# Two small evictions and a negation moved from ScalarE to VectorE in a fused convolution and gated MLP with gradients

## The chip, the cores and the metric

The kernel runs on one core of one Trainium2 chip, in one launch. The time is the device time in microseconds. Before the change it is 517.62 us, the median of three runs (517.49 to 518.38). A core has five engines that run side by side, each through its own instructions in order: TensorE (PE in the profile, with its weight loads as PEld), VectorE (DVE), ScalarE (ACT), GpSimd (POOL) and SyncE (SP, which here only starts transfers).

## The reference

The kernel computes one forward pass and the gradients of nine of its inputs. Sequence length S is 2048, width D is 512, inner width F is 1376, all in bf16.

```
xn = layernorm(A_q)
k_shift[t] = sum over lag 0..3 of k[t - lag] * shift_k[:, lag]
kv = k_shift * v
y  = causal convolution of kv with ssm_k along S (FFT of length 4096) + kv * ssm_D
s  = xn * y
h  = sigmoid(xn @ w_gate) * (xn @ w_up)
g  = silu(h @ w_down)
out = A_q + s * g
```

It returns `out` and, for a given `grad_out`, the gradients for A_q, A_k, A_v, A_shift_k, A_ssm_k, A_ssm_D, w_gate, w_up and w_down. The gradients of the convolution are convolutions as well, so they need a forward transform of the gradient of `y`, products with the spectra of `kv` and `ssm_k`, and inverse transforms.

## The kernel before

**Tiles.** The sequence is cut into NJ = 16 tiles of 128 positions, and position p * 16 + j lies on partition p of tile j. The width is cut into 4 groups of 128 channels (`cg`). The tiles go through the MLP in the order SEQ, which begins 15, 13, 11, 9; `POS[i]` is the place of tile i in it, so `POS[i] < 2` means tiles 15 and 13.

**Stages.** In the first stage (up to about 160 us) four streams are interleaved: `strG` runs the gate and up projections of nine tiles (`f_gen`), `strK` and `strV` make the spectra of `ssm_k` and `kv`, and `strX` multiplies them and transforms back. The second stage (`stepB`, up to about 355 us) does the rest of the MLP and its backward pass, tile by tile. In the last stage `frontC` transforms the gradient of `y`, `backC` makes the two products and their inverse transforms for each channel group, and `dW` computes the three weight gradients as long accumulations of matmuls (into PSUM tiles of their own), which fill TensorE between the others.

**A tile's projections.** `f_ln` computes a tile's statistics on VectorE with a power on GpSimd, and writes the normalised tile to `xnA`. `f_xt` transposes it: for the places 0 to 3 and 9 to 11 of SEQ with four 128x128 matmuls against the identity into a PSUM tile of the kind "tr", of which there are two, then an eviction to `xnT` (line 732); for the others with a DMA. `f_gen` multiplies the weights with `xnT` in three blocks of 32, 32 and 24 matmuls. The projections of tile 15 wait for the weights, which are loaded in three pieces; the first block of tile 13 uses the same first piece as that of tile 15.

**An eviction.** `evac` (line 238) records a copy from PSUM to SBUF with two alternatives, ScalarE or VectorE.

**The last stage's spectra.** For each group and each quarter `qq` of its channels `step3T` makes a spectrum by two matmuls into a PSUM tile of 1024 columns (two banks), with the real parts on one half of the partitions and the imaginary parts on the other. From it come two SBUF tiles: `Xc`, the spectrum itself (`dst`), and `Xw`, the same with the halves swapped and one negated (`sw`). In this stage such 1024-wide PSUM tiles come from two slots (kind "mm2c"), which all steps of the transforms share. A slot is free once its last reader is done. Lines 958 to 960:

```python
        nc.evac(v(dst), pv[:], 1024)
        nc.scalar.copy(v(sw[0:64]), pv[64:128])
        nc.scalar.mul(v(sw[64:128]), pv[0:64], -1.0)
```

`backC` then makes four products on VectorE (lines 1353 to 1355), for t = 0 and 1: `PP[t]` from `Xc`, and `KK[t]` from `Xw`, in place over the loaded spectra. Two `inv3` calls follow, each of 16 matmuls: the first takes `PP[0]` and `KK[0]`, the second `PP[1]` and `KK[1]`.

**What sets the order.** No instruction is issued where it is written. The class `Rec` records all of them, the streams being interleaved by `run_streams` by shares of their work. `order` then plays the whole program through a cost model of the engines, the transfers and the PSUM slots, and gives each engine its order: of the operations that are ready, the one that was recorded first goes first. At the same place it chooses the engine of an eviction, VectorE only if ScalarE is behind by a margin. So a changed cost or a fixed engine at one place changes the order and the choices at many later ones. All instructions are emitted on line 522, which is why every line of the profile names it; groups are told apart by engine, operation and shape.

Of the kernel before, what the change touches and what calls it, by code (L numbers as in the profile page):

```python
# [9 lines left out]
ALU = mybir.AluOpType  # L10
# [27 lines left out]
POS = {i: n for n, i in enumerate(SEQ)}  # L38
# [598 lines left out]
def kernel_impl(ctx, tc, A_q, A_k, A_v, A_shift_k, A_ssm_k, A_ssm_D, B_x, B_w_gate, B_w_up, B_w_down,  # L637
                grad_out, out_0, out_1, out_2, out_3, out_4, out_5, out_6, out_7, out_8, out_9):
    nc = tc.nc
# [18 lines left out]
    def ps_mm(shape, dt=f32, name=None):  # L658
        return nc.ps(PS["mm"], shape, dt)
# [4 lines left out]
    def ps_tr(shape, dt=bf16, name=None):  # L664
        return nc.ps("tr", shape, dt)
# [25 lines left out]
    T = [dict() for _ in range(NJ)]  # L691
# [31 lines left out]
    def f_xt(i):  # L723
        if POS[i] > 3 and not 8 < POS[i] < 12:
            T[i]["xnT"] = xnT_r.next()
            nc.sync.dma_start_transpose(T[i]["xnT"], xnA[:, i, :])
            return
        pt = ps_tr([4, 128], name="ps_xnT")
        for db in range(4):
            nc.tensor.transpose(pt[:, db, :], xnA[:, i, db * 128:(db + 1) * 128], ident)  # L730
        T[i]["xnT"] = xnT_r.next()
        nc.evac(T[i]["xnT"], pt[:], 512)

    def f_gen(i):
        xnT = T[i]["xnT"]
# [129 lines left out]
    f_ln(SEQ[0])  # L865
    next(consts)
    f_xt(SEQ[0])
    f_ln(SEQ[1])
    next(consts)
# [74 lines left out]
    def step3T(Qf, rows, qq, dst, sw):  # L944
        if rows:
            ps = ps_mm([64, 8, 2], name="ps_x")
            for h in range(2):
                src = Qf.rearrange("p (k g) -> p k g", g=64)[:, 32 * h:32 * h + 32, 16 * qq:16 * qq + 16]
                nc.tensor.matmul(ps[:, 32 * h:32 * h + 32].rearrange("p k g x -> p k (g x)"), BDq, src, start=True, stop=True)
            pv = ps.rearrange("p k g x -> p g k x")  # L950
            v = lambda a: a.rearrange("p (g k x) -> p g k x", g=8, x=2)
        else:
            pv = ps = ps_mm([1024], name="ps_x")
            for h in range(2):
                o = 1024 * qq + 512 * h
                nc.tensor.matmul(ps[:, h * 512:(h + 1) * 512], BDq, Qf[:, o:o + 512], start=True, stop=True)
            v = lambda a: a
        nc.evac(v(dst), pv[:], 1024)
        nc.scalar.copy(v(sw[0:64]), pv[64:128])
        nc.scalar.mul(v(sw[64:128]), pv[0:64], -1.0)  # L960

    def inv3(parts, qq, Bg, rows=False):
        ps = ps_mm([8, NJ, 8], name="ps_b")
# [346 lines left out]
    def ld_KK(n):  # L1310
        if n < 16:
            KK = KK_r.next()
            nc.sync.dma_start(KK, KK_d[n // 4, n % 4].rearrange("t p x -> p t x"))
            stC["KK", n] = KK
# [10 lines left out]
    def ld_bwd(cg):  # L1325
        c0, c1 = cg * GW, (cg + 1) * GW
        if cg % 2 == 0:
            stC["vg"] = vg_r.next()
            nc.sync.dma_start(stC["vg"], vC[:, :, c0:c0 + 256])
        ksh, kh = ksh_r.next(), kh_r.next()  # L1330
        nc.sync.dma_start(ksh.rearrange("p j d -> p (j d)"), ksh_d[cg])
        nc.gpsimd.memset(kh[0:1, 0:3, :], 0.0)
        nc.sync.dma_start(kh[:, 3:, :], kC[:, :, c0:c1])
        ld_halo(nc.sync, kh[:, 0:3, :], kHalo[:, 0:3, c0:c1])
        stC["bwd", cg] = (ksh, kh)

    def backC():
        for cg in range(NG):
            c0, c1 = cg * GW, (cg + 1) * GW
            B1, B2 = B1_r.next(), B2_r.next()  # L1340
            ys = {}
            for qq in range(5):
                if qq < 4:
                    n = cg * 4 + qq
                    while ("Qf", cg) not in stC:
                        yield 0
                    Xc, Xw = Xc_r.next(), Xw_r.next()
                    step3T(stC["Qf", cg], cg > 1, qq, Xc, Xw)
                    stC["nY"] = n + 1
                    yield 1024  # L1350
                    KK = stC.pop(("KK", n))
                    PP = P_r.next()
                    for t in range(2):
                        nc.vector.tensor_tensor(PP[:, t], Xc, KK[:, t], ALU.mult)
                        nc.vector.tensor_tensor(KK[:, t], Xw, KK[:, t], ALU.mult)
                    ys[qq] = (PP, KK)
                if qq == 2:
                    ld_bwd(cg)
                if qq > 0:
                    PP, KK = ys.pop(qq - 1)  # L1360
                    inv3([(PP[:, 0], RC1), (KK[:, 0], RS2)], qq - 1, B1)
                    yield 2048
                    inv3([(PP[:, 1], RC1), (KK[:, 1], RS2)], qq - 1, B2, True)
                    ld_KK(cg * 4 + qq + 2)
                    yield 2048
            dkv = y2A[:, :, c0:c1]
            yield from inv1(B1, dkv)
            ksh, kh = stC.pop(("bwd", cg))
            vg = stC["vg"][:, :, (cg % 2) * GW:(cg % 2 + 1) * GW]
            dks = dks_r.next()  # L1370
            nc.vector.tensor_tensor(dks[:, 0:NJ, :], dkv, vg, ALU.mult)
            nc.vector.memset(dks[96:P, NJ:NJ + 3, :], 0.0)
            nc.gpsimd.dma_start(dks[0:112, NJ:NJ + 3, :], dks[1:113, 0:3, :])
            nc.gpsimd.dma_start(dks[112:127, NJ:NJ + 3, :], dks[113:128, 0:3, :])
            nc.vector.tensor_tensor(dkv, dkv, ksh, ALU.mult)
            dKT = ar.view(B1_r.blks[0][0], [128, NJ], bf16)
            Bv = B2.rearrange("p j e g c -> p j (e g) c")
            for jh in range(2):
                pk = ps_mm([8, 128], name="ps_dk")
                for jj in range(8):  # L1380
                    j = 8 * jh + jj
                    for c in range(2):
                        nc.tensor.matmul(pk[:, jj, :], Bv[:, j, :, c], Ci[:, c, j, :], start=(c == 0), stop=(c == 1))
                nc.evac(dKT[:, :, 8 * jh:8 * jh + 8], pk[:].rearrange("p j n -> p n j"), 1024)
                yield 2048
            nc.sync.dma_start(out_5[c0:c1, :], dKT.rearrange("p n j -> p (n j)"))
            if cg % 2 == 1:
                nc.sync.dma_start(o3C[:, :, c0 - GW:c1], y2A[:, :, c0 - GW:c1])
            nc.vector.tensor_copy(dDo[:, cg:cg + 1], dKT[:, 0, 0:1])
            pa = ps_tr([4, 32], f32, name="ps_diag")  # L1390
            for j in range(NJ):
                for e in range(4):
                    es = slice(32 * e, 32 * e + 32)
                    nc.tensor.matmul(pa[es], dks[:, j, es], kh[:, j:j + 4, es], start=(j == 0), stop=(j == NJ - 1))
                if j == 7:
                    yield 2048
            nc.vector.tensor_tensor(dm, pa[:], id32[:, None, :].to_broadcast([P, 4, 32]), ALU.mult)
            nc.vector.tensor_reduce(res[:, cg, :], dm, AX.X, ALU.add)
            yield 2048
            if cg % 2 == 0:  # L1400
                stC["dk"] = dk_r.next()
            dk = stC["dk"][:, :, (cg % 2) * GW:(cg % 2 + 1) * GW]
            for lag in range(4):
                src = dks[:, lag:lag + NJ, :]
                skl = skb[:, lag:lag + 1, c0:c1].to_broadcast([P, NJ, GW])
                if lag == 0:
                    nc.vector.tensor_tensor(dk, src, skl, ALU.mult)
                else:
                    term = term_r.next()
                    nc.vector.tensor_tensor(term, src, skl, ALU.mult)  # L1410
                    yield 512
                    nc.vector.tensor_tensor(dk, dk, term, ALU.add)
                yield 512
            if cg % 2 == 1:
                nc.sync.dma_start(o2C[:, :, c0 - GW:c1], stC["dk"])
        for lag in range(4):
            nc.vector.tensor_copy(skout[:, :, lag:lag + 1], res[:, :, 3 - lag:4 - lag])
        po = ps_tr([GW, 4], f32)
        for t in range(4):
            nc.tensor.matmul(po[0:4, :, t], skout[:, :, t], ident, start=True, stop=True)  # L1420
        nc.evac(row4[0:4, :], po[0:4].rearrange("p a t -> p (a t)"), 512)
        nc.sync.dma_start(out_4.rearrange("(g p) t -> g (p t)", p=P), row4[0:4, :])
        pd = ps_tr([GW], f32)
        nc.tensor.matmul(pd[0:4, :], dDo, ident, start=True, stop=True)
        nc.evac(row6[0:4, :], pd[0:4], 128)
        nc.sync.dma_start(out_6.rearrange("(g p) -> g p", p=P), row6[0:4, :])
# [116 lines left out]
```

## Time and profile before

| | |
|---|---|
| time | 517.62 us |
| span of the profiled run | 516.4 us |
| TensorE busy | 489.1 us, 95% |
| VectorE busy | 387.6 us, 75% |
| ScalarE busy | 353.2 us, 68% |
| GpSimd busy | 136.7 us, 26% |
| granted TensorE clock | 1.0 |
| data moved | 112.92 MB, 219 GB/s |
| ScalarE, negation of a half spectrum, 64x1024 f32 from PSUM | 16, 1.015 us each |
| ScalarE, copy of a half spectrum, 64x1024 f32 from PSUM | 16, 1.008 us each |
| ScalarE, eviction of 128x1024 f32 in the last stage | 69, 1.024 us each |
| VectorE, eviction of 128x1024 f32 in the last stage | 7, 1.219 us each |
| VectorE, product 128x1024 bf16 in the last stage | 64, 0.687 us each |

The busy time of an engine is the time in which at least one of its instructions ran. A group's line gives the engine, the operation, what it writes and reads, the shapes, the count, the busy time and the mean of one, and then the idle time just before these instructions with what ended it. A stretch in the timeline is a run of instructions without a gap; the idle time before it stands in brackets. Loss on an engine counts only where TensorE, or what it waits for, is held up by it.

### The profile page before, as it was taken

The numbers are of one execution on the slowest core, as the hardware profiler recorded it, in microseconds if no ns is written. First come the engines' busy times: TensorE is split into PE (matmuls) and PEld (weight loads), VectorE is DVE, ScalarE is ACT, GpSimd is POOL, SyncE is SP. The second block draws the span as 40 slices with busy tenths as digits, with TensorE's granted clock in tenths as the row PEclk, the third lists the DMA queues.
The fourth block names the chain that finished last, engine by engine and source line by source line (L and its number), as shares of the span: only waits on it lengthen the run. The fifth ranks groups of instructions, "written<-read, shape, count | busy, mean of one in ns | idle before, by whom it ended". The sixth has DMA issues, their size and how long they took to land.

```text
span 516.4 us, 13503 instructions
## 1 busy us (share of the span) xinstructions
PE 489.1 (95%) x5379; PEld 350.0 (68%) x5437; DVE 387.6 (75%) x768; ACT 353.2 (68%) x471; POOL 136.7 (26%) x257
## 2 busy tenths in 40 slices
PE   4789899899899999999999999999999999999997
PEld 3678798889787676666666556644675675866644
DVE  8799998877648779867779998436759859698440
ACT  7799999988975564455545546326878988786611
POOL 7255634444413432424153511000010010010000
PEclk9999999999999999999999999999999999999999
DMA  8989996698999655737499956989699699999973
GB/s 208 310 265 282 317 329 211 189 289 193 218 200 211 176 171 135 222 110 196 115 244 233 243 181 164 231 286 235 149 218 268 175 268 300 211 242 240 211 200 100
DMA packets 176888, 112.92 MB, mean 219 GB/s; under 512 B 126587, under 2 KB 160985, under 8 KB 176570
## 3 DMA queue, kind: packets, MB, share of 16 engines
q1 hardware_dynamic: 164424, 76.54, 63.5%
q0 software_dynamic: 11872, 35.53, 21.9%
q8 instruction: 42, 0.69, 0.6%
q14 instruction: 20, 0.16, 0.1%
q10 hardware_dynamic: 530, 0.01, 0.1%
HBM read 37.65 MB, written 45.72 MB: 161 GB/s over the span
## 4 chain that ended last, share of the span: by engine, by line
PE 77%; ACT 9%; DVE 7%; issue 4%; DMA 2%; POOL 1%; ACTq 0%; DVEq 0%; POOLq 0%
PE psum L522 77%; ACT slab L522 9%; DVE slab L522 7%; DMA slab<-in_A_q_dram 1%; DMA slab<-in_A_ssm_D_dram 1%; POOL slab L522 1%; POOL hF_d L522 0%; ACTq L522 0%; DVEq L522 0%; POOLq L522 0%
## 5 line engine op out<-in xcount | busy, mean ns | idle before, releaser
L522 PE MATMUL psum<-slab 128*128 128x128 bf16 (+4 forms) x5379 | 489.1, 254 | 24.2 <-ACT slab L522 10.1
L522 PEld LDWEIGHTS <-slab 128*128 128x128 bf16 (+1 forms) x5437 | 350.0, 99 | 163.0 <-issue 15.8
L522 DVE TENSOR_TENSOR slab<-slab 128x512 bf16<-128x512 bf16 (+6 forms) x488 | 268.9, 601 | 53.1 <-ACT slab L522 45.8
L522 ACT CAST slab<-psum 128x1024 bf16<-128x1024 f32 (+5 forms) x276 | 224.5, 867 | 91.1 <-PE psum L522 81.4
L522 ACT ACTIVATE slab<-psum 128x512 bf16<-128x512 f32 (+2 forms) x80 | 55.2, 694 | 38.9 <-PE psum L522 35.6
L522 ACT ACTIVATE slab<-slab 128x512 bf16<-128x512 bf16 (+3 forms) x71 | 56.8, 810 | 15.2 <-DVE slab L522 13.9
L522 ACT COPY slab<-psum 128x1024 bf16<-128x1024 bf16 (+1 forms) x42 | 39.2, 987 | 13.5 <-PE psum L522 13.5
L522 POOL DMA_DIRECT2D out_dram<-slab x32 | 17.4, 545 | 95.4 <-DVE slab L522 95.4
L522 POOL DMA_DIRECT2D slab<-slab x8 | 4.3, 544 | 130.9 <-DVE slab L522 130.6
L522 DVE TENSOR_TENSOR slab<-psum,slab 128x512 bf16<-128x512 f32 (+2 forms) x47 | 29.4, 627 | 10.6 <-ACT slab L522 7.7
L522 POOL DMA_DIRECT2D hF_d<-slab x48 | 26.2, 547 | 30.7 <-DVE slab L522 30.0
L522 DVE SCALAR_TENSOR_TENSOR slab<-psum,slab 128x512 bf16<-128x512 f32 x16 | 11.1, 691 | 27.1 <-PE psum L522 27.1
L522 DVE CAST slab<-psum 128x1024 bf16<-128x1024 f32 (+1 forms) x18 | 20.2, 1131 | 4.1 <-PE psum L522 4.0
L522 POOL DMA_DIRECT2D KK_d<-slab x32 | 17.4, 546 | 17.0 <-ACT slab L522 15.5
L522 POOL DMA_DIRECT2D slab<-in_A_q_dram x29 | 16.1, 556 | 11.0 <-DVE slab L522 4.8
L522 DVE SCALAR_TENSOR_TENSOR slab<-slab 128x512 bf16<-128x512 bf16 (+3 forms) x41 | 17.1, 416 | 0.8
L522 DVE STREAM_TRANSPOSE slab<-slab 128x1024 f32<-128x1024 f32 x8 | 14.3, 1834 | 4.0 <-ACT slab L522 4.0
L522 DVE TENSOR_SCALAR slab<-slab 128x1 f32<-128x1 f32 (+9 forms) x48 | 12.1, 268 | 6.3 <-POOL slab L522 5.4
L522 POOL TENSOR_TENSOR slab<-slab 128x1 f32<-128x1 f32 x16 | 9.8, 615 | 14.0 <-DVE slab L522 13.8
L522 POOL DMA_DIRECT2D slab<-hF_d x18 | 9.7, 541 | 12.2 <-PE psum L522 10.1
L522 DVE BATCH_NORM_STATS2 slab<-slab 128x6 f32<-128x512 bf16 x16 | 10.9, 686 | 0.5 <-DMA slab<-in_A_q_dram 0.5
L522 POOL DMA_DIRECT2D slab<-in_grad_out_dram x16 | 8.6, 540 | 7.6 <-DMA out_dram<-slab 7.1
(23 smaller groups left out, 48.9 us busy)
## 6 DMA issues: line engine op xcount, KB each, us to landing
KK_d<-slab POOLq DMA_DIRECT2D x32, 256.0 KB, 5.0
slab<-KK_d SPq DMA_DIRECT2D x16, 512.0 KB, 4.7
slab<-in_A_k_dram SPq DMA_DIRECT2D x8, 512.0 KB, 6.3
hF_d<-slab POOLq DMA_DIRECT2D x32, 128.0 KB, 4.0
slab<-slab SPq DMA_DIRECT2D x32, 128.0 KB, 4.7
out_dram<-slab POOLq DMA_DIRECT2D x32, 128.0 KB, 3.1
uF_d<-slab SPq DMA_DIRECT2D x32, 128.0 KB, 2.4
gF_d<-slab SPq DMA_DIRECT2D x32, 128.0 KB, 2.6
```

Source lines behind the costliest of these rows:

```text
L522: getattr(getattr(self.nc, eng), meth)(*[place(v) for v in a], **{x: place(v) for x, v in k.items()})
```

## The change

Three edits. The eviction of the transposed activations of the first two tiles is fixed to VectorE, in place of the planner's choice (before, ScalarE evicted tile 15 and VectorE tile 13). The negated half of `Xw` is made by VectorE from `Xc` in SBUF, in place of ScalarE from PSUM: it takes work from ScalarE and makes the half copy the last reader of the PSUM tile beside the eviction. And the two products that need only `Xc` are recorded ahead of the two that need `Xw`, so that VectorE has something to do while the swapped half is made.

```diff
@@ f_xt
         T[i]["xnT"] = xnT_r.next()
-        nc.evac(T[i]["xnT"], pt[:], 512)
+        if POS[i] < 2:
+            nc.vector.tensor_copy(T[i]["xnT"], pt[:])
+        else:
+            nc.evac(T[i]["xnT"], pt[:], 512)
@@ step3T
         nc.evac(v(dst), pv[:], 1024)
         nc.scalar.copy(v(sw[0:64]), pv[64:128])
-        nc.scalar.mul(v(sw[64:128]), pv[0:64], -1.0)
+        nc.vector.tensor_scalar(sw[64:128], dst[0:64], -1.0, None, ALU.mult)
@@ backC
                     for t in range(2):
                         nc.vector.tensor_tensor(PP[:, t], Xc, KK[:, t], ALU.mult)
+                    for t in range(2):
                         nc.vector.tensor_tensor(KK[:, t], Xw, KK[:, t], ALU.mult)
```

## The prediction

> **What bounds the kernel now.** I read the page's busy shares first, then the busy time of the engines stage by stage, then TensorE's stretches and waits in the places that the change touches.
>
> ```profile
> PE 489.1 (95%) x5379; PEld 350.0 (68%) x5437; DVE 387.6 (75%) x768; ACT 353.2 (68%) x471; POOL 136.7 (26%) x257
> ```
>
> TensorE is busy for 489.1 of 516.4 us, so all that can be won by moving work between the other engines is its 27.3 us of idleness. The stage table says where that lies (columns: stretch, its length, busy us of PE, PEld, DVE, ACT, POOL).
>
> ```profile
> 0.00:40.00 40.00, 28.31 (x355) 24.12 (x358) 34.21 (x84) 32.54 (x44) 21.49 (x45) 1.00 0.95 264
> 40.00:80.00 40.00, 37.31 (x580) 33.89 (x585) 37.28 (x53) 39.99 (x49) 19.40 (x35) 1.00 0.92 299
> 80.00:120.00 40.00, 37.64 (x588) 34.19 (x590) 33.58 (x50) 36.41 (x44) 17.36 (x33) 1.00 0.77 230
> 120.00:160.00 40.00, 36.90 (x558) 32.86 (x562) 24.20 (x47) 31.22 (x44) 15.19 (x30) 1.00 1.10 201
> ```
>
> 11.7 us are idle in the first 40, 2.7 + 2.4 + 3.1 = 8.2 us up to 160. From 40 to 80 ScalarE never stops (39.99 of 40): there it sets the pace and TensorE follows. From 160 to 355 TensorE idles for 1.05 us in 195, and nothing can be won. From 355 on it is idle for 6.4 us, of which 3.1 are the tail after 500.
>
> TensorE's own stretches show the first wait that the change is after (start, length, count, and in brackets the idle time before it and who ended it):
>
> ```profile
> 14.50 4.33 PE L522 MATMUL psum<-slab 128*128 128x128 bf16 x48 [0.33 <-ACT slab L522]
> 19.05 1.05 PE L522 MATMUL psum<-slab 128*128 128x128 bf16 x16 [0.22 <-ACT slab L522]
> 22.14 11.03 PE L522 MATMUL psum<-slab 128*128 128x128 bf16 x162 [2.04 <-DVE slab L522]
> ```
>
> VectorE in the same time shows what TensorE waited for:
>
> ```profile
> 17.70 1.29 DVE L522 BATCH_NORM_STATS2 slab<-slab 128x6 f32<-128x512 bf16 x2 [0.47 <-DMA slab<-in_A_q_dram]
> ...
> 20.74 0.69 DVE L522 TENSOR_TENSOR slab<-psum,slab 128x512 bf16<-128x512 f32 x1 [0.34 <-issue]
> 21.35 0.40 DVE L522 TENSOR_SCALAR slab<-slab 128x512 bf16<-128x512 bf16 x1
> 21.67 0.42 DVE L522 COPY slab<-psum 128x512 bf16<-128x512 bf16 x1
> ```
>
> The copy of 21.67 is the eviction of the second tile's transposed activations; it ends at 22.09, TensorE goes on at 22.14. Its transposes had been made by 11.9, but on VectorE it stands behind two statistics, the first held for a load, and a product. In the planned order two matmuls of tile 13 stand ahead of 16 of tile 15, and block them.
>
> In the last stage the waits that end on ScalarE are these (the first line is the sum over 355 to 516.4):
>
> ```profile
> PE psum L522 <- ACT slab L522: 2.1, 5, 0.5
> ```
>
> ```profile
> 361.82 6.13 PE L522 MATMUL psum<-slab 128*128 128x128 bf16 x62 [0.46 <-ACT slab L522]
> 368.35 4.68 PE L522 MATMUL psum<-slab 128*128 128x128 bf16 x44 [0.41 <-ACT slab L522]
> 373.45 6.73 PE L522 MATMUL psum<-slab 128*128 128x128 bf16 x95 [0.41 <-ACT slab L522]
> ```
>
> ```profile
> 360.75 1.01 ACT L522 ACTIVATE slab<-psum 64x1024 bf16<-64x1024 f32 x1
> 367.29 1.01 ACT L522 ACTIVATE slab<-psum 64x1024 bf16<-64x1024 f32 x1
> 372.38 1.01 ACT L522 ACTIVATE slab<-psum 64x1024 bf16<-64x1024 f32 x1
> ```
>
> Each wait ends 0.05 to 0.06 us after such an ACTIVATE ends (361.76, 368.30, 373.39). The same holds of the other two, at 427.69 and 476.02. That instruction is the negation the change moves; it is the last reader of the half spectrum's PSUM tile, and only two such tiles exist in this stage.
>
> **What the Trainium skill says.** "ScalarE: Activation LUTs", section "What ACT_TABLE_LOAD costs": an ACTIVATE with immediate scale and bias costs 186 ns + 0.833 ns per element, 1039 ns for 1024. The trace agrees: 1015 ns for the negation on 64 partitions, 1024 ns for a whole eviction on 128; half the partitions save nothing. "VectorE: DVE Perf Modes", section "The perf-mode tier table": a one-source operation on bf16 in SBUF runs at four elements per cycle, a two-source one at two. The trace has the second (687 ns for a 128x1024 product, the 2x price), but not the first: its bf16 128x512 TENSOR_SCALAR, with a scalar for each partition, takes 411 ns, the price of two per cycle. Same page, section "Two Vector instructions with no wait between them": an operation whose input or output starts in another quadrant of partitions than the last waits until all before it have finished. The negation writes partition 64 on, its neighbours partition 0 on. The trace has no such pair; what it shows is the overlap that would be lost: two products of 0.687 us take 1.29 together, 0.08 less than their sum.
>
> **Part 1, the two evictions on VectorE.** Tile 15: ScalarE loses a copy (128x512 bf16 COPY, 0.58 to 0.61 us), VectorE gets one of 0.42. In the built order it stands between the first table's products, where VectorE waited for GpSimd until 10.80 (its normalisation of tile 13), so it delays only the tables' chain, by up to 0.4; the first weights are there at 14.38 in any case (TensorE's weight load waited 1.19 us for them). Cost on the path: 0 to 0.3, I take 0.1. Tile 13: already on VectorE, but in the built order it now stands right after the table arithmetic, ahead of all three statistics. That arithmetic ended at 16.2; with 0.4 of delay the copy is done near 17.0. TensorE reaches tile 13's matmuls when its 48 are through, at 18.83, and 32 of them stand ahead of the second block of tile 15. The weights for these have been used by tile 15 already, so they run 2.0 us (32 at 0.061), just as long as the hole was. The hole of 2.04 goes, less 0.1 and what the next PSUM wait takes: 1.8 at this spot.
>
> Does that reach the end? ScalarE was idle for 2.48 us before 23.80 for want of TensorE, and paces the stretch to 80; starting earlier, it takes the gain along. Besides, the planner's choice of engine moves in the first stage: by the built order VectorE gets 15 instead of 12 bf16 evictions of 128x1024 (0.684 each) and 11 instead of 8 f32 ones (1.22), +5.7 us, and ScalarE loses six of about 1.05, -6.3 us. Over 40 to 160 that leaves both below TensorE in sum, but VectorE (37.28 of 40) is as full as ScalarE was. The order of nearly everything between 30 and 160 is new, so its 8.2 us of idleness are dealt again; I see no reason for a sign and put +-1.5 on it. First stage: -1.5 us, from -3.2 to +0.8.
>
> **Part 2, the negation on VectorE.** Removed: 16 ACTIVATEs of 1.015 = 16.2 us of ScalarE between 355 and 500, where it is busy for 111.3 of 145. By the built order ScalarE takes back four evictions of 1024 (7 become 3 on VectorE) and two of 512: +4.1 + 1.2. Net -10.9. Added to VectorE: 16 TENSOR_SCALAR of 64x1024. Low end by the tier table's rate, (150 + 256 cycles)/0.96 = 0.42 us; high end by the 2x price, 0.69 (the product's row); and up to 0.16 for the overlap lost on both sides. I take 0.6, since the trace leaves the fourfold rate open: 9.6 us, less 4 x 1.22 + 2 x 0.684 = 6.2: +3.4 on 107.2 of 145. VectorE is 97% full from 385 to 400 and from 460 to 470, but there weight gradients fill TensorE, and such filler runs on alone from 500 to 513, so a product that comes 1 or 2 us later shifts filler and not the end.
>
> What waits anew: the negation waits for the eviction on ScalarE (about 1.02 us), and behind it on VectorE stand the swapped products, for which the inverse matmuls wait. Before: eviction, copy and negation are 3 x 1.02 = 3.1 us before the first swapped product. After: copy at 2.0; on VectorE the two unswapped products and the negation, 1.0 + 1.29 + 0.6 = 2.9. Hardly earlier, so that path gains 0.2, or loses 0.1 at the high price. The PSUM tile is free at 2.0 and not 3.1, and that ends the five waits: 0.46 + 0.41 + 0.41 + 0.37 + 0.41 = 2.06. I let 0.9 come back as waits for VectorE: last stage -1.2 us, from -2.1 to +1.0.
>
> **Part 3, unswapped products first.** The same 64 products; it lets two of each four start without the swapped half. No cost; its gain is counted above.
>
> **Sum.** -1.5 - 1.2 = -2.7: 517.62 - 2.7 = 514.9.
>
> **Rivals.**
> A: only the first wait goes, and the inverse matmuls wait for the negation as long as before: 517.6 - 1.5 = 516.1. For it: the path to the swapped product is as good as unchanged. Against: all five waits end with the PSUM tile's last reader.
> B: the new order of the first stage gives its gain back (ScalarE's pace from 40 to 80 replaced by VectorE's, three more strided evictions of 1.22): 517.6 - 1.2 = 516.4, or with the last stage's gain halved too 517.0. For it: 37.28 of 40. Against: ScalarE's 2.48 us of lost time are won for it.
> C: slower. The negation at 0.85 with the held neighbours, planned for less, makes the inverse matmuls wait: 16 x 0.25 = 4 us, half of it hidden by filler, +2.0, with +0.8 from a poor first stage less the 2.06 of freed waits: 518.3. For it: three-quarters of VectorE is in use, and it is in order. Against: filler up to the end.
>
> **How the numbers follow.** Forecast 0.50 (513 to 515.8), A 0.18, B 0.17, C 0.15. All of the forecast's cases and most of A and over half of B lie below 516.6 (0.2% under): faster 0.76. Same: the rest of B, a little of A and a third of C, 0.13. Slower 0.11. Range: from both gains full with a lucky order, 512.8, to near C's middle, 518.0.
>
> **What would show it.** TensorE's hole of 2.04 us before tile 13 gone, and its stretch from 14.5 unbroken to about 28; ScalarE without the 2.48. No ACTIVATE of 64x1024 in the last stage, 16 TENSOR_SCALAR of 64x1024 at 0.42 to 0.69, the five waits on ScalarE gone, new ones on VectorE under 0.9 in sum. Wrong if the idle time of TensorE from 28 to 160 grows by over 1.5 us, or if TensorE waits in the last stage for VectorE by 2 us or more.

## The result

The changed kernel takes 513.22 us (median of 4 runs, 513.04 to 514.92), the kernel before on the same chip 517.74 (4 runs, 517.49 to 518.38). The ratio is 0.9918, with a 95% interval of 0.9895 to 0.9941: 4.2 us saved, between 3.1 and 5.4. A second measurement of both gave less, with an interval that overlaps the first: 0.9942 (0.9919 to 0.9964), 3.0 us saved.

First the busy shares on the page of the changed kernel, and its stage table (the same columns as before).

```profile
PE 493.9 (96%) x5437; PEld 352.7 (69%) x5437; DVE 392.9 (77%) x785; ACT 338.4 (66%) x454; POOL 136.2 (27%) x257
```

```profile
0.00:40.00 40.00, 30.75 (x364) 26.35 (x365) 34.62 (x85) 31.17 (x41) 20.92 (x45) 0.96 0.96 273
40.00:80.00 40.00, 37.09 (x568) 33.32 (x567) 38.08 (x54) 38.27 (x45) 19.34 (x33) 1.00 0.93 276
80.00:120.00 40.00, 38.29 (x592) 34.40 (x590) 36.14 (x53) 35.80 (x43) 19.12 (x34) 1.00 0.78 237
120.00:160.00 40.00, 39.34 (x608) 35.20 (x605) 26.83 (x55) 32.37 (x47) 15.32 (x30) 1.00 1.13 227
```

ScalarE lost 14.8 us and VectorE gained 5.3. TensorE seems busier than before, 493.9 against 489.1, with the same matmuls: the trace of before holds 5379 of the 5437, so part of the 27.3 us that I read there as idle was missing records. A kernel with the order of before but for one copy, and a full trace (`pin_copy13` below), idles for 516.2 - 493.9 = 22.3 us. That is the number to compare with; the changed kernel idles for 19.2 us, and for 20.4 in the second measurement (512.4 - 492.0).

TensorE's timeline from 14 us on shows the hole before tile 13 gone: a single stretch of 284 matmuls, where before 48, 16 and 162 stood with 2.04 us between. VectorE's copy is now done by 17.1.

```profile
14.19 19.50 PE L522 MATMUL psum<-slab 128*128 128x128 bf16 x284 [1.27 <-DMA slab<-in_B_w_gate_dram]
34.27 1.10 PE L522 MATMUL psum<-slab 128*128 128x128 bf16 x16 [0.58 <-ACT slab L522]
```

```profile
16.68 0.42 DVE L522 COPY slab<-psum 128x512 bf16<-128x512 bf16 x1
```

The negation, among VectorE's groups of the last stage, takes 0.421 us; the evictions of 1024 columns beside it have become three, from seven.

```profile
L522 DVE TENSOR_TENSOR slab<-slab 128x1024 bf16<-128x1024 bf16 x64 | 40.4, 686 | 3.1 <-ACT slab L522 2.5
L522 DVE TENSOR_SCALAR slab<-slab 64x1024 bf16<-64x1024 bf16 x16 | 6.7, 421 | 0.5
L522 DVE CAST slab<-psum 128x1024 bf16<-128x1024 f32 x3 | 3.7, 1222 | 1.8 <-PE psum L522 1.7
```

And TensorE's waits from 345 us on, which before were 2.1 us in five, all on ScalarE, are now (us in total, times, longest):

```profile
PE psum L522 <- ACT slab L522: 1.2, 3, 0.6
PE psum L522 <- DVE slab L522: 0.4, 1, 0.4
```

To place the gain I use two marks. VectorE makes sixteen SCALAR_TENSOR_TENSOR of 128x512 that read PSUM, one for each tile of the second stage; the start of the first closes the first stage, that of the sixteenth opens the last.

| kernel | first mark | second mark | second mark to the end |
|---|---|---|---|
| before | 170.31 | 343.47 | 172.9 |
| changed | 168.49 | 341.65 | 171.5 |
| changed, second measurement | 166.76 | 340.88 | 171.5 |

Between the marks nothing was won; the second measurement lost 1.0 us there. The last stage gave 1.4 us, the first stage 1.8 in the first measurement and 3.6 in the second.

How far can such marks be trusted from one trace each? TensorE's order in the first stage is the same in four traces below, and their first marks lie between 168.95 and 170.09; six have the order of the changed kernel, and lie between 166.76 and 168.49. The last stage of before, in the same order on TensorE, VectorE and ScalarE, took 172.9 to 173.3 us in four traces, and 174.3 in one (`bias2`); that of the changed kernel 171.5, 171.5 and 171.8 in three. So a gap of 1 us in one trace is not sure.

### The profile page after: what moved, and what is told of

The parts are those of the page before. It is cut to its first block, busy times and chain, and to the rows that moved or that the text cites. A ratio compares the mean times of both kernels' runs of the same rounds, so it can differ in the third digit from the quotient of the medians.

```text
span 513.1 us, 13560 instructions
## 1 busy us (share of the span) xinstructions
PE 493.9 (96%) x5437; PEld 352.7 (69%) x5437; DVE 392.9 (77%) x785; ACT 338.4 (66%) x454; POOL 136.2 (27%) x257
## 4 chain that ended last, share of the span: by engine, by line
PE 78%; DMA 5%; issue 5%; DVE 4%; POOL 3%; ACT 2%; SPq 1%; POOLq 0%; ACTq 0%; DVEq 0%
PE psum L522 78%; DVE slab L522 4%; ACT slab L522 2%; DMA slab<-in_grad_out_dram 2%; DMA slab<-in_B_w_gate_dram 1%; DMA slab<-slab 1%; SPq L522 1%; POOL slab L522 1%; POOL hF_d L522 1%; POOL KK_d L522 1%; DMA slab<-in_A_ssm_k_dram 1%; POOL ksh_d L522 0%; POOL sF_d L522 0%; POOLq L522 0%; ACTq L522 0%
## 5 line engine op out<-in xcount | busy, mean ns | idle before, releaser
L522 PE MATMUL psum<-slab 128*128 128x128 bf16 (+2 forms) x5437 | 493.9, 256 | 16.2 <-DVE slab L522 9.1
L522 DVE TENSOR_TENSOR slab<-slab 128x512 bf16<-128x512 bf16 (+7 forms) x488 | 267.8, 600 | 48.1 <-ACT slab L522 38.2
L522 ACT CAST slab<-psum 128x1024 bf16<-128x1024 f32 (+4 forms) x279 | 224.7, 839 | 100.6 <-PE psum L522 89.0
L522 ACT ACTIVATE slab<-slab 128x512 bf16<-128x512 bf16 (+3 forms) x71 | 56.7, 808 | 16.1 <-DVE slab L522 14.8
L522 ACT ACTIVATE slab<-psum 128x512 bf16<-128x512 f32 (+1 forms) x64 | 37.5, 588 | 38.5 <-PE psum L522 38.3
L522 ACT COPY slab<-psum 128x1024 bf16<-128x1024 bf16 (+1 forms) x38 | 34.3, 936 | 15.0 <-PE psum L522 15.0
L522 DVE TENSOR_SCALAR slab<-slab 128x512 bf16<-128x512 bf16 (+10 forms) x64 | 18.7, 306 | 3.0 <-POOL slab L522 1.6
L522 DVE CAST slab<-psum 128x1024 bf16<-128x1024 f32 (+1 forms) x15 | 17.8, 1184 | 4.0 <-PE psum L522 2.5
L522 DVE SCALAR_TENSOR_TENSOR slab<-slab 128x512 bf16<-128x512 bf16 (+3 forms) x41 | 17.1, 416 | 0.8
L522 POOL TENSOR_TENSOR slab<-slab 128x1 f32<-128x1 f32 x16 | 11.0, 687 | 11.4 <-DVE slab L522 11.3
L522 DVE COPY slab<-psum 128x1024 bf16<-128x1024 bf16 (+1 forms) x19 | 11.7, 629 | 2.1 <-PE psum L522 1.5
```

The costliest lines, as they stand in the source:

```text
L522: getattr(getattr(self.nc, eng), meth)(*[place(v) for v in a], **{x: place(v) for x, v in k.items()})
```

## The experiments

Ratios are to the kernel before, measured on the same chip, with 95% intervals. Of longer edits only the lines that act are shown.

**One half of the change each.** `evict_only` is part 1 alone: the kernel before with the two evictions fixed to VectorE.

```diff
-        nc.evac(T[i]["xnT"], pt[:], 512)
+        if POS[i] < 2:
+            nc.vector.tensor_copy(T[i]["xnT"], pt[:])
+        else:
+            nc.evac(T[i]["xnT"], pt[:], 512)
```

> Only the two evictions fixed to VectorE. Theory (the hole before tile 13 was the loss, and ScalarE's pace passes the gain on): -1.8 us at the end of the first tile's backward pass, as in the changed kernel (168.5 instead of 170.3), nothing in the last stage: 515.9. Rival (the gain of the first stage needs ScalarE's relief elsewhere or a lucky order): under 0.5 us, 517.2 or more.

514.87 us, ratio 0.9948 (0.9930 to 0.9966): -2.7 us. First mark 166.80, last stage 172.9, as before. That is more than either theory had.

`neg_only` is the rest: negation on VectorE and the new order of the products.

> The negation on VectorE and the unswapped products first, evictions as before. The first stage's order should be that of before, so its marks stay at 170.3 and 343.5. Theory (the freed PSUM tile ends the five waits of 2.06 us in sum): -1.5 to -2.5 us, 515.2 to 516.2. Rival (VectorE's waits take their place and the last stage gains nothing): 517.3 or more.

516.59 us, ratio 0.9982 (0.9972 to 0.9992): -0.9 us, between what the two theories had. First mark 169.66, last stage 171.8, or 1.2 less than before. And the changed kernel measured anew beside them:

> The changed kernel once more, on the chip that the other runs of this group use. Every theory expects 513.2 us, a ratio of 0.991 to 0.992 to the kernel before. Its first profile ran TensorE at half clock from 37 to 40.3 us; if that stretch is not part of the kernel, this one's span is 511.4 instead of 513.1.

514.61 us, ratio 0.9942, and a span of 512.4 where 511.4 was expected. The halves add up to -2.7 - 0.9 = -3.6, between the two measurements of the whole. The sum is not tight: beside the whole, measured in the same group, `evict_only` is only 0.26 us slower, so what parts 2 and 3 add on top of part 1 is seen in the traces and in `neg_only`, and not in this pair of times. Part 1 is worth more than I gave it, and all of it falls before the first mark.

**Does closing the hole bring it?** `pin_copy13` keeps the order of the kernel before on all engines and takes one instruction forward: the copy of tile 13 on VectorE, to right behind the table arithmetic, where the changed kernel has it.

```diff
         seq = self.order()
+        k = next(n for n, r in enumerate(seq) if r[0] is self.m13)
+        r = seq.pop(k)
+        seq.insert(1 + next(n for n, r in enumerate(seq) if r[0] is self.mAN), r)
```

`m13` is that copy and `mAN` the last operation of the table arithmetic, both noted where they are recorded.

> The kernel before with its order kept instruction by instruction, except that VectorE's eviction of tile 13's transposed activations stands right after the table arithmetic instead of behind the statistics and the product. Theory (the hole of 2.04 us alone): the hole closes and most of it arrives, -1.2 to -2.0 us: 515.7 to 516.5. Rival (a new order of the whole first stage made the gain): the hole closes, but ScalarE's pace from 40 to 80 us eats it: under 0.5 us, 517.2 or more.

517.22 us, ratio 0.9996 (0.9981 to 1.0010): nothing that can be measured. The hole is closed all the same. TensorE's timeline:

```profile
14.68 10.46 PE L526 MATMUL psum<-slab 128*128 128x128 bf16 x131 [0.33 <-ACT slab L526]
26.00 6.94 PE L526 MATMUL psum<-slab 128*128 128x512 bf16 x97 [0.86 <-DVE slab L526]
33.26 0.61 PE L526 MATMUL psum<-slab 128*128 128x128 bf16 x8 [0.33 <-ACT slab L526]
```

The 131 matmuls run without a gap, and at 26 stands a new wait of 0.86. What ends it is on VectorE's timeline of the same kernel: the next tiles' normalisation waits for GpSimd's powers, 1.72 and 0.90 us.

```profile
23.02 0.41 DVE L526 TENSOR_SCALAR slab<-slab 128x512 bf16<-128x512 bf16 x1 [1.72 <-POOL slab L526]
23.35 0.68 DVE L526 TENSOR_TENSOR slab<-psum,slab 128x512 bf16<-128x512 f32 x1
24.93 0.41 DVE L526 TENSOR_SCALAR slab<-slab 128x512 bf16<-128x512 bf16 x1 [0.90 <-POOL slab L526]
25.26 0.68 DVE L526 COPY slab<-psum 128x1024 bf16<-128x1024 bf16 x1
```

The stretch that began at 33.71 before begins at 33.26: of 2.04 us 0.45 are left there, and at the first mark 0.2 (170.09 against 170.31).

**Each copy alone.** `tile13_only` and `tile15_only` fix one of the two evictions (`POS[i] == 1`, `POS[i] == 0`) and let the planner go on from there.

> Only tile 13's eviction fixed to VectorE. By the built order it stands early, 32 matmuls of tile 13 run ahead of tile 15's second block, and VectorE takes 20 large evictions of the first stage as before (26 in the kernel with both evictions). Theory E (the early work that fills TensorE is the gain): as with both evictions, -2 to -3 us, 514.8 to 515.6. Theory R (ScalarE's relief by six evictions is the gain): under 0.7 us, 516.9 or more. Theory L (the gain is whatever the new order happens to give): anywhere from -2 to +1 us.

> Only tile 15's eviction fixed to VectorE. By the built order tile 13's is late as before, behind the statistics, one matmul of tile 13 blocks TensorE, and VectorE takes 20 large evictions of the first stage. Theory E: nothing, 517.3 to 517.8. Theory R: under 0.7 us, 516.9 or more. Theory L: anywhere from -2 to +1 us.

518.63 and 518.78 us, ratios 1.0005 (0.9987 to 1.0023) and 1.0004 (0.9988 to 1.0020). In the first TensorE is as early as in the changed kernel: one stretch of 250 matmuls from 14.54, and no idle time at all from 20 to 26. Yet its first mark is 169.29. So an early start is not enough; of these orders only that with both copies wins.

**Does relief of ScalarE bring it?** `bias2` is the kernel before with a planner that prefers VectorE in the first stage, so that VectorE takes 24 large evictions there and not 20, without the edit.

```diff
         op.bias = 0.3 if esize(src.ap.dtype) == 2 else 0
+        if self.late == 1 << 30:
+            op.bias += 0.2
```

> The kernel before with no eviction fixed; in the first stage the planner's margin for giving an eviction to VectorE is 0.2 larger. By the built order VectorE takes 24 large evictions of the first stage instead of 20, and 14 matmuls of tile 13 run ahead of tile 15's second block, then one blocks. Theory R: -1.5 to -2.5 us, 515 to 516. Theory E: -0.5 to -1.5 us. Theory L: anywhere from -2 to +1 us.

523.62 us, ratio 1.0103 (1.0066 to 1.0140): 5.3 us slower. TensorE idles for 8.9 us between 80 and 170. Its two longest waits there don't end on ScalarE: 2.12 us for VectorE at 146, and 3.02, until 170.4, for a load of `w_up`. So neither the early start nor the relief of ScalarE is enough by itself. That the relief has no part in the gain isn't shown, since this order is another one altogether.

**Where the first stage gains.** These traces are complete. Four kernels have the first-stage order of before (`pin_copy13`, but for the one copy, `neg_only`, and `pin_neg` and `order_only` below), six that of the changed kernel (both its measurements, `evict_only`, and three below). TensorE's idle time, as a mean, worked out as stretch less busy time:

| us | 0 to 33 | 33 to 45 | 45 to 80 | 80 to 170 | first mark |
|---|---|---|---|---|---|
| order of before (4) | 9.25 | 1.08 | 2.25 | 4.29 | 169.5 |
| order of the changed kernel (6) | 7.30 | 3.02 | 2.05 | 1.97 | 167.3 |

The lead of 1.95 us from the closed hole is given back in the next twelve. (Of the six, four ran TensorE at half clock for 3.4 us between 36 and 41, and slower matmuls count as busy; the two others idle for 7.1 up to 33 and 3.9 from there to 45, so they give back more than the lead.) What stays is the 2.3 us after 80. Most of it lies in a few waits, on TensorE's timeline of `pin_copy13`:

```profile
121.18 15.59 PE L526 MATMUL psum<-slab 128*128 128x128 bf16 x261 [0.23 <-ACT slab L526]
137.02 1.70 PE L526 MATMUL psum<-slab 128*128 128x512 bf16 x19 [0.25 <-DVE slab L526]
139.67 1.11 PE L526 MATMUL psum<-slab 128*128 128x128 bf16 x17 [0.94 <-ACT slab L526]
142.07 30.14 PE L526 MATMUL psum<-slab 128*128 128x512 bf16 x378 [1.29 <-ACT slab L526]
```

and are not there in `evict_only`, where one stretch runs to the end of the stage:

```profile
119.49 52.72 PE L522 MATMUL psum<-slab 128*128 128x128 bf16 x752 [0.17 <-ACT slab L522]
```

The longest of them is no shortage of ScalarE. Its eviction, for which TensorE waits at 142.07, itself waits for a store of products to `KK_d`, on ScalarE's timeline of `pin_copy13`:

```profile
141.00 1.50 ACT L526 CAST slab<-psum 128x1024 bf16<-128x1024 f32 x2 [1.39 <-DMA KK_d<-slab]
```

All five traces with this order, that of before too, have the same: the store, issued near 135, takes 4.8 to 5.8 us, and the eviction starts 0.10 us after it has landed. (In two of them the view names TensorE as what ended ScalarE's wait; the landing shows that it was the store.) TensorE's wait varies with it, 1.29 here and 0.39 in `pin_neg`. The 0.94 before it is another matter: it ends with an eviction, and ScalarE had been busy without a pause from 131 on. In the new order no wait for that store reaches TensorE. Which of the moves in that order does it can't be told from these runs.

**The negation without new planning.** `pin_neg` keeps the order of the kernel before on every engine, products included, and takes each negation out of ScalarE's queue and puts it at the same place of the common order on VectorE.

```diff
-                eng, meth, a, k = op.alts[q]
+                eng, meth, a, k = self.neg.get(op.n, op.alts[q])
...
         nc.scalar.mul(v(sw[64:128]), pv[0:64], -1.0)
+        nc.neg[nc.ops[-1].n] = ("vector", "tensor_scalar", (sw[64:128], dst[0:64], -1.0, None, ALU.mult), {})
```

> The instruction order of the kernel before is kept on every engine; only the 16 negations of the last stage are taken from ScalarE and put at the same place of the common order on VectorE, reading the finished SBUF half. No other engine choice is planned anew, and the products stay swapped and unswapped in turn. Theory (the PSUM tile freed one ACTIVATE earlier is what ends the five waits): the waits of TensorE on ScalarE in the last stage fall from 2.1 us to under 0.8 without any new planning, and the time falls by 0.5 to 1.5 us, less what the negation adds on VectorE ahead of the swapped products. Rival (the gain of the last stage comes from the planner's dealing the evictions anew and from the order of the products): the time is unchanged or up to 1.5 us longer, with new waits of TensorE for VectorE in place of those on ScalarE.

517.58 us, ratio 0.9993 (0.9985 to 1.0001): nothing that can be measured. Last stage 173.1. All five waits on ScalarE are gone, and six on VectorE have come:

```profile
PE psum L523 <- DVE slab L523: 3.0, 6, 0.7
```

Both halves of that can be dated. `pin_copy13` and `pin_neg` issue the same matmuls in the same order; in the 60 us after the second mark TensorE runs 510 in the one and 533 in the other. Then VectorE, busy for 19.17 of the 20 us from 420 on (18.96 in `pin_copy13`) and still with its old share of large evictions besides the negations, lets TensorE wait at 409 and five times from 435 to 459, among them:

```profile
436.08 0.23 PE L523 MATMUL psum<-slab 128*128 128x128 bf16 x1 [0.66 <-DVE slab L523]
436.87 3.63 PE L523 MATMUL psum<-slab 128*128 128x128 bf16 x39 [0.57 <-DVE slab L523]
440.94 16.48 PE L523 MATMUL psum<-slab 128*128 128x256 bf16 x225 [0.44 <-DVE slab L523]
```

**The order of the products.** `neg_noorder` is the changed kernel with part 3 taken back; `order_only` is part 3 alone.

```diff
                         nc.vector.tensor_tensor(PP[:, t], Xc, KK[:, t], ALU.mult)
-                    for t in range(2):
                         nc.vector.tensor_tensor(KK[:, t], Xw, KK[:, t], ALU.mult)
```

> The changed kernel with the four products in their old order (unswapped and swapped by turns). The first stage is that of the changed kernel. Theory (the recorded order only decides between products that are ready at once): 0 to +0.5 us to the changed kernel, 513.3 to 514.3. Rival (the second unswapped product hides the negation, and without it VectorE waits about 0.7 us in each of 16 quarters, a part of it reaching TensorE): +1 to +2 us.

> Part 3 alone: the kernel before with both unswapped products ahead of both swapped ones, the negation still on ScalarE. Theory (the order pays only because the negation on VectorE delays the swapped half): no difference within 0.4 us, last stage about 172.9 us from the last spectrum product to the end. Rival (the order pays by itself, since the swapped half comes late from ScalarE as well): 0.7 to 1.5 us shorter, last stage about 171.8 us.

`neg_noorder` takes 515.99 us, ratio 0.9950 (0.9926 to 0.9973), with a last stage of 173.6: 2.1 us longer than with part 3, and 0.7 longer than before the change. The times alone don't separate it from the changed kernel, whose second measurement gave 0.9942; nor from `evict_only` with 0.9948, so part 2 without part 3 shows no gain in time. TensorE waits 1.6 us for ScalarE and 1.1 for VectorE. By the traces, the theory that part 3 brings nothing fell. `order_only` takes 522.05 us, ratio 1.0073 (1.0047 to 1.0099), last stage 176.0: 3.0 us longer. Neither theory had that. Most of it is one wait, on TensorE's timeline:

```profile
463.90 16.07 PE L522 MATMUL psum<-slab 128*128 128x512 bf16 x133 [2.97 <-ACT slab L522]
```

and ScalarE's timeline shows what it is queued behind. Two spectra are taken there in one go, with evictions, halves and negations, 5.2 us without a pause, and only then comes the eviction of 352 columns that TensorE needs:

```profile
458.21 2.04 ACT L522 CAST slab<-psum 128x1024 bf16<-128x1024 f32 x2 [2.43 <-PE psum L522]
460.28 1.01 ACT L522 ACTIVATE slab<-psum 64x1024 bf16<-64x1024 f32 x1
461.32 1.01 ACT L522 CAST slab<-psum 64x1024 bf16<-64x1024 f32 x1
462.35 1.02 ACT L522 ACTIVATE slab<-psum 64x1024 bf16<-64x1024 f32 x1
463.39 0.81 ACT L522 CAST slab<-psum 128x352 bf16<-128x352 f32 x2
```

So by itself part 3 loses 3.0 us in this stage, and part 2 wins nothing (0.7 longer in its trace, which is within what one order spreads); together they win 1.2 to 1.4.

**PSUM hold or ScalarE's load?** Two twins of the changed kernel have an extra copy of 64x1024 on ScalarE, 16 times, into a scratch tile that nobody reads. In `dummy_psum` it reads the PSUM tile, as the old negation did; in `dummy_sbuf` the finished half in SBUF.

```diff
         nc.scalar.copy(v(sw[0:64]), pv[64:128])
+        nc.scalar.copy(v(stC["dm"][0:64]), pv[0:64])       # dummy_psum
+        nc.scalar.copy(v(stC["dm"][0:64]), v(dst[0:64]))   # dummy_sbuf
```

Each twin has one of the two lines; the scratch tile's allocation isn't shown.

> The changed kernel with an extra copy on ScalarE of the 64x1024 half of the PSUM tile that the negation used to read, into a scratch tile nobody reads: ScalarE carries the 16 instructions again, and the PSUM tile is held as long as before, while the negation stays on VectorE. Theory (hold of the PSUM tile): the last stage gets 1.0 to 2.0 us longer than in the changed kernel, and TensorE's waits on ScalarE there are back at about 2 us. Rival (load of ScalarE): the same, so that only the twin run tells them apart; if nothing of 0.5 us or more comes back, neither holds and the gain lay in the planner's dealing.

> The twin: the same extra ScalarE copy of 64x1024, but read from the finished SBUF half and not from PSUM, so that ScalarE carries the load and the PSUM tile is free early. Theory (hold of the PSUM tile): under 0.6 us longer than the changed kernel, waits of TensorE on ScalarE in the last stage about 1.2 us as there. Rival (load of ScalarE): as slow as the twin that reads PSUM, 1.0 to 2.0 us longer.

515.16 us, ratio 0.9951 (0.9934 to 0.9967), last stage 173.3; and 516.47 us, ratio 0.9971 (0.9957 to 0.9985), last stage 173.7. Against 171.5 both lose about 2 us in this stage; in time the first can't be told from the second measurement of the changed kernel (0.9942), the second is 1.5 us behind it. The waits are not alike. With the PSUM tile held:

```profile
PE psum L522 <- ACT slab L522: 2.2, 4, 0.8
PE psum L522 <- DVE slab L522: 0.4, 1, 0.4
```

with the load alone:

```profile
PE psum L522 <- DMA slab<-uF_d: 1.1, 1, 1.1
PE psum L522 <- ACT slab L522: 0.7, 2, 0.4
PE psum L522 <- DVE slab L522: 0.6, 1, 0.6
```

That the hold of the tile makes the waits on ScalarE agrees with this: 2.2 us with it, 0.7 without. But the theory that only the hold counts fell. The twin with the load alone loses as much, in other places: the planner gives VectorE six of the large evictions there and not three, and a transfer comes 1.1 us late at 504. I did not follow that transfer back to its cause. Both twins were planned anew, so how much of a loss is the copy itself and how much the new dealing isn't separated.

The last stage in one table (idle: TensorE from 345 to 500; the waits of TensorE are from 345 on; the last column counts the 128x1024 evictions on VectorE):

| kernel | second mark to end | idle | waits on ScalarE / VectorE / DMA | evictions |
|---|---|---|---|---|
| pin_copy13 (stage as before) | 172.9 | 2.09 | 2.1 / 0 / 0 | 7 |
| changed | 171.5 | 1.64 | 1.2 / 0.4 / 0 | 3 |
| neg_only | 171.8 | 1.69 | 1.2 / 0.4 / 0 | 3 |
| pin_neg | 173.1 | 2.97 | 0 / 3.0 / 0 | 7 |
| neg_noorder | 173.6 | 2.91 | 1.6 / 1.1 / 0 | 4 |
| order_only | 176.0 | 5.03 | 5.0 / 0 / 0 | 7 |
| dummy_psum | 173.3 | 2.71 | 2.2 / 0.4 / 0 | 4 |
| dummy_sbuf | 173.7 | 1.69 | 0.7 / 0.6 / 1.1 | 6 |

## Why the prediction came out, step by step

514.9 was forecast, 513.2 and 514.6 measured. The sum was nearly right; one of its two terms, that of the first stage, for the wrong reason, and there the hit was luck.

**"The hole of 2.04 goes, less 0.1 and what the next PSUM wait takes: 1.8 at this spot."** The hole went, but this step failed in what follows from it: "ScalarE ... paces the stretch to 80; starting earlier, it takes the gain along." It does not. `pin_copy13` closes the hole and gains 0.2 us in its trace and nothing in its time. I took ScalarE's 39.99 of 40 for a pace that starts whenever ScalarE starts. In `pin_copy13` it is the chain of statistics, GpSimd's powers and normalisations that lets work start after the hole; and before the change the trace's chain of work that ended last ran from 17 to 26 us through it, and not through the hole.

**"The order of nearly everything between 30 and 160 is new ... I see no reason for a sign and put +-1.5 on it."** This is where all of part 1 lies: -2.3 us at the first mark (169.53 to 167.25, means of the four and the six traces), most of it in the waits of 121 to 142. -1.5 was forecast for the stage, from -3.2 to +0.8. The size was inside; the term that carried it was booked as noise. That no sign could be given was fair: two other redealt orders were worth nothing (each tile alone) and a third cost 5.3 us.

**Tile 15's 0.1 and the copies' price.** The copy took 0.42 us as said. No cost on the path can be seen: TensorE is busy for 12.5 to 13.2 us in the first 20 in both measurements of the changed kernel, against 12.1 in `pin_copy13`.

**The negation, 0.6 taken between 0.42 and 0.69.** Mis-sized: it is 0.421 us. "VectorE: DVE Perf Modes", section "The perf-mode tier table", in the Trainium skill has `tensor_scalar` on bf16 in SBUF at four elements per cycle; with that rate my low end was 0.42, and the trace agrees. I had leaned on the 411 ns of a bf16 128x512 TENSOR_SCALAR, which makes two operations, each with a scalar for every partition; here that was no measure for one operation with a constant. VectorE in the last stage went from 112.5 to 113.2 us from 345 on (112.6 in the second measurement), +0.7 at most and not +3.4.

**"I let 0.9 come back as waits for VectorE: last stage -1.2 us."** Measured -1.4, in `neg_only` -1.2. The five waits do end, shown without any new planning by `pin_neg`; what comes back is 1.6 us of visible waits and not 0.9 (1.2 on ScalarE in three other places, at 368, 437 and 472, which the prediction didn't have, and 0.4 on VectorE). By visible waits the gain is only 2.09 - 1.64 = 0.45 us of idle time. The other 1.0 lies inside the stretches: the same 1635 matmuls after the second mark keep TensorE busy for 167.74 us in `pin_copy13`, 166.98 in `pin_neg` in the very same order, and 166.74 in the changed kernel. So delays count as busy time there, since the profile models the ends of matmuls; what makes them stays open.

**"No cost; its gain is counted above" (part 3).** Too small. Part 2 without part 3 has a last stage of 173.6 us, no shorter than before; with part 3 it is 171.5. How much of the 2.1 us is the order of the products itself, and how much the planner's dealing the evictions with it, isn't separated: a fixed order with both parts wasn't tried.

**The rivals.** A (inverse matmuls wait for the negation as long as before) is close to what `pin_neg` shows. B (the new first stage gives its gain back) is true of the hole's gain, but another took its place. C did not happen.

## What to carry to other kernels

A hole on the busiest engine is worth what the chain behind it allows: before booking it, follow who releases the work after it, and try the one instruction in an order that is otherwise fixed. Where a planner deals the order anew, a small edit can be mostly a draw from that planner (here -2.7, 0, 0 and +5.3 us for four of them), so measure the edit apart from the draw. Work moved to another engine needs room there in the same stage: here the negation won only in the kernels in which the evictions were dealt anew and VectorE had unswapped products to do meanwhile.

## What the runs showed of the hardware

In the profile of the changed kernel TensorE ran at half its clock for 3.3 us, with nothing like it in the second measurement of the same kernel. From the table of stretches (the column before the last two is the granted clock):

```profile
37.00:40.30 3.30, 3.27 (x21) 2.12 (x20) 3.23 (x8) 2.02 (x2) 2.63 (x5) 0.50 1.10 316
```

```profile
33.00:45.00 12.00, 8.17 (x114) 6.72 (x114) 11.37 (x15) 10.94 (x13) 6.19 (x9) 1.00 0.96 284
```

Both had waits of 0.54 to 0.61 us there, between short stretches. "TensorE: Matmul & The Clock Gate", section "What's actually happening", in the Trainium skill has the clock halved after at least one idle window of about 3.4 us, in windows that run regardless of the kernel. Eight of the fourteen traces have one such stretch of 3.41 us before 45 us: this one, `evict_only`, both twins and `bias2` near 36 to 41, `pin_neg`, `tile13_only` and `tile15_only` between 15 and 24. In none of them was the window before it idle: TensorE was busy for 1.10 to 1.96 of its 3.41 us, and in the changed kernel no wait in it was longer than 0.61. So the traces ask less than a wholly idle window. Busy time alone doesn't decide it either: in `bias2` a window from 165.9 with 1.48 us busy was followed by the full clock. That the stretch struck one execution of the changed kernel and not the other agrees with windows that run by themselves.

In `evict_only`, whose matmuls come in the same order there, the stretch from 37.4 to 40.8 cost nothing that can be seen. Its TensorE ran the same 62 matmuls slower and waited less, and went on with the next ones at the same time as in the second measurement of the changed kernel (first two lines `evict_only`, then the changed kernel):

```profile
37.02 5.58 PE L522 MATMUL psum<-slab 128*128 128x128 bf16 x62 [0.22 <-DVE slab L522]
43.36 2.84 PE L522 MATMUL psum<-slab 128*128 128x128 bf16 x48 [0.76 <-DVE slab L522]
```

```profile
37.00 2.33 PE L522 MATMUL psum<-slab 128*128 128x128 bf16 x30 [0.22 <-DVE slab L522]
40.20 1.95 PE L522 MATMUL psum<-slab 128*128 128x128 bf16 x32 [0.87 <-DVE slab L522]
43.33 2.84 PE L522 MATMUL psum<-slab 128*128 128x128 bf16 x48 [1.19 <-DVE slab L522]
```
